# Threshold attention and SwiGLU on one core: two more products by blocks of 128 in the third chunk, and other ranks behind the last scores

## The chip, the cores and the metric

The kernel runs on one core of a Trainium2 chip, in fp32 throughout. The time is that of the device for one launch, in microseconds (us). The core has a matrix engine (PE, with its weight loads shown apart as PEld), three engines for elementwise work (DVE, ACT and POOL), and SP, which only issues DMAs here. Each engine takes its instructions in the order in which the program gives them, and waits for others by semaphores. Matmul results land in PSUM, in eight banks of 128 x 512 fp32; everything else lives in SBUF, 128 partitions wide.

## The reference

```python
# q, k, v: (8, 8, 576, 64)
scores = (1.0 / np.sqrt(64)) * np.matmul(q, k.transpose(0, 1, 3, 2))
thresh = np.max(scores, axis=-1, keepdims=True) - tau
scores = np.where(scores >= thresh, scores, -1000000000.0)
scores = scores - np.max(scores, axis=-1, keepdims=True)
attn = np.exp(scores)
attn = attn / (np.sum(attn, axis=-1, keepdims=True) + 1e-09)
attn_out = np.matmul(attn, v)
x = attn_out.transpose(0, 2, 1, 3).reshape(4608, 512)
g = x @ w_gate                       # (512, 1536)
silu = g * (1.0 / (1.0 + np.exp(-g)))
val = x @ w_val                      # (512, 1536)
out = silu * val @ w_out             # (1536, 512)
```

So per batch there are eight heads of attention with a mask at the row's maximum less tau, and then a feed-forward block over all 4608 tokens.

## The kernel before

**Tokens in chunks.** The feed-forward block works on nine chunks of 512 tokens, `c` = 0 to 8. Chunks 0 to 7 are the first 512 tokens of each batch; chunk 8 (`B` in the code) is made of the last 64 tokens of all batches. The first chunks use plain products, the others seven products in place of eight (Strassen and Winograd forms: sums of the operands' quarters, seven products, sums of these). "Third chunk" is `c` = 2, which the code calls `DEEP`.

**Scores and attention.** Heads go by pairs (`seg`), three tiles of queries to a pair; one tile is one slot, twelve slots to a batch. In a slot `slot_scores` (L2058) writes the scores of a tile into the PSUM tiles `sc`; `slot_rest` then takes the rows' maxima (DVE L2079, L2081), the exponential (ACT L2104), the mask with its row sums (DVE L2106), exchanges sums between partitions (ACT L2115, the job `xj`), adds them up and takes the reciprocal (DVE L2120 and L2121, `rj`), scales six parts (ACT L2133, or POOL L2130 as many times as the table `POOLED` says for this slot) and transposes (DVE L2135). `attend` (L2157) multiplies by v a slot later; PE's next score tile waits for the masks of the one before, since these free the `sc` tiles.

**Gates and values.** While batch b's scores run, `block_part(b, kk)` gives PE the feed-forward work of chunk c = b − 1, so many steps a slot (`GV`). For each of six groups g of 256 columns, `gates_and_values` runs seven products, p1 to p7, of 128 x 128 weights with 256 tokens, four matmuls each (`Group.mul`, L1138). The chunk's two halves of 256 tokens go together: with p3 the first half of the group is complete, with p4 the second, and `finish` then takes tanh and the products with the value. `NestedGroup` does p5 and p3 each as seven products again, of blocks of 128 x 128 tokens (L1333): seven matmuls into two banks, `Seven.fill` (ACT L1271 for 384 columns and L1273 for 512) brings them to SBUF, and `Seven.fold` puts them together with four adds on DVE or POOL, as `FOLDS` says by group (all such adds show as L929 on DVE and L926 on POOL). The weights' sums for it are loaded with the group's other weights, the tokens' sums are made once per chunk by `deepen_x`, four adds on DVE. Which groups take `NestedGroup` is said by `WITH_BLOCKS` = (1, 2, 3) and by the chunk.

**Outputs.** `Deep` multiplies gated values by w_out, again by seven products: `early` and `late` make the sums s1, s2, s3 of the gated values (128x512 each, `sum`), `inner_sums` makes four sums of 128x384 of one operand o for the products inside product o, `nested` is these inner products (L1768, banks px or py), two outer products are flat (L1777). `combine` puts inner products together (four adds big<-big,px on DVE behind an ACT copy), `ship` stores the result (L1829). `deepen(o)` prepares weights, four adds of 128x384 on POOL each.

**Behind the last scores** (`tail[0]` is true) chunks 7 and 8 remain. For each group g the class `Whole` runs the seven products of both chunks, all by blocks (L2543): `folded` brings four of them together on DVE, p3 and p7 add to what `fill` left (DVE L2615, L2625), `fold` runs on POOL, and `finish` takes tanh (ACT L2593), the product with the value (DVE L2595) and an end product by DVE or POOL. Chunk 8's gated values go to HBM (`hall_hbm`, L2608) and are loaded again (L2669) after chunk 7's outputs begin, since their place is still in use. Then the outputs of chunk 7, `Deep(B - 1)`, and of chunk 8, `Deep(B)`, end the kernel.

**The order of the work.** PE's order is the order of the calls. The order on DVE, ACT, POOL and SP is fixed while the program is built, by the class `Plan`: every piece of work is a job with an engine, an estimated duration (`took`), a rank and the jobs that it depends on; at every point of PE's planned time, each engine takes the ready job of least rank, then the one that was ready first. `lag` delays the planned end for those that depend on the job. So a changed rank, lag or engine changes the written order on every engine that follows; the hardware then holds to that order, whatever is ready.

```python
n = min((i for i, j in enumerate(jobs) if j.ready <= start + (0.0 if j.rank else self.PATIENCE)),
        key=lambda i: (self.rank(jobs[i], start), jobs[i].ready, i))
```

Of the kernel before, what the change touches and what calls it, by code (L numbers as in the profile page):

```python
# [14 lines left out]
ALU = mybir.AluOpType  # L15
# [129 lines left out]
def kernel(  # L145
# [13 lines left out]
    B, H, S, D = q.shape  # L159
# [13 lines left out]
    NU3 = 3  # L173
# [4 lines left out]
    NF2, DM2 = NF // 2, DM // 2  # L178
# [50 lines left out]
    NESTED = 0, 1, 6  # L229
# [622 lines left out]
    plan = Plan()  # L852
# [62 lines left out]
    DEEP = 2  # L915
# [345 lines left out]
    class Seven(Buf):  # L1261
# [13 lines left out]
        def fold(self, eng, rank, *deps):  # L1275

            y = self.place.rearrange("p (x q) -> p x q", q=P)
            tt, took, less = (dve_tt, 0.36, 0.23) if eng == "DVE" else (pool_tt, 0.85, 0.52) if tail[0] else (pool_tt, 0.75, 0.44)
            twice = lambda x: y[:, x:x + 1].broadcast_to((P, 2, P))
            j = job(eng, took, tt(y[:, 1:3], twice(0), y[:, 1:3], ALU.add), *deps, rank=rank)  # L1280
            j = job(eng, took, tt(y[:, 0:7:6], twice(2), y[:, 5:7], ALU.add), j, rank=rank)
            j = job(eng, less, tt(y[:, 2], y[:, 0], y[:, 3], ALU.add), j, rank=rank)
            return job(eng, took, tt(y[:, 4:6], twice(6), y[:, 4:6], ALU.add), j, rank=rank)

    class Flat:

# [388 lines left out]
    class Deep:  # L1675
# [37 lines left out]
            self.sixth_place = xall[:, 2 * KW:3 * KW]  # L1713
            self.sixth_sums(mark)

        by_pool = False

        def second_of_s1(self):
            self.by_pool = True
            x = NF2 // 2 - 2  # L1720
            self.ready["s1"].append(self.sum(self.a21, self.a21, self.a22, ALU.add, x, self.ready["s3"][x], gated[self.c, 1, NF2 - 2]))

# [10 lines left out]
        def sum(self, out, a, b, op, x, *deps, rank=2):  # L1733
            fs = slice(2 * x, 2 * x + 2)
            tt, eng, took = (dve_tt, "DVE", 0.62) if tail[0] else (pool_tt, "POOL", 1.3)
            rank = min(rank, 1) if tail[0] else rank
            if self.by_pool and not self.in_outputs:
                tt, eng, took = pool_tt, "POOL", 1.3
            return job(eng, took, tt(out[:, fs], a[:, fs], b[:, fs], op), *deps, rank=rank)

        def inner_sums(self, o, a, place, ready, *deps):

            a11, a21, a12, a22 = quarters(a)
            flat = place if len(place.shape) == 2 else place.rearrange("p f n -> p (f n)")
            s1, s2, s3, s4 = (flat[:, n * QW:(n + 1) * QW].rearrange("p (f q) -> p f q", q=P) for n in range(4))
            tt, eng, took = (dve_tt, "DVE", 0.55) if tail[0] else (pool_tt, "POOL", 1.0)
            rank = 0 if o == 1 and self.c == B - 1 else 0 if o == 1 else 1 if o == 5 or o in (3, 6) and not tail[0] or o in (0, 6) and tail[0] or self.c == B - 2 else 2
            j3 = job(eng, took, tt(s3, a11, a21, ALU.subtract), *ready, *deps, rank=rank)
            j1 = job(eng, took, tt(s1, a21, a22, ALU.add), *ready, *deps, j3, rank=rank)
            j2 = job(eng, took, tt(s2, s1, a11, ALU.subtract), j1, rank=rank)  # L1750
            j4 = job(eng, took, tt(s4, a12, s2, ALU.subtract), j2, rank=rank)
            self.inner[o] = [(a11, ready), (a12, ready), (s4, [j4]), (a22, ready), (s1, [j1]), (s2, [j2]), (s3, [j3])]
# [310 lines left out]
    def slot_rest(seg, t, pss, mark, pooled, max_by_act, rank):  # L2063
# [50 lines left out]
                o = g ^ 1  # L2114
                nc.scalar.copy(sm[g * G:(g + 1) * G, 0:m, 1], sm[o * G:(o + 1) * G, 0:m, 0])  # L2115

        xj = job("ACT", 0.78, exchange, *masks.values(), rank=1)

        def total():
            nc.vector.tensor_reduce(out=tot[:, 0:m], in_=sm[:, 0:m, :], axis=AX.X, op=ALU.add)  # L2120
            nc.vector.reciprocal(out=ri[:, 0:m], in_=tot[:, 0:m])  # L2121

        rj = job("DVE", 0.36, total, xj, rank=1)
        sum_users[-1].append(rj)
        for u in range(NU3):
            scaled = []
# [99 lines left out]
    def gates_and_values(c):  # L2226

        old = None
        settled[0] = c >= DEEP
        while u_bufs[0] is not u_list[0]:  # L2230
            u_bufs.rotate(-1)
        for g in range(NF2):
            deep = c > DEEP and g in WITH_BLOCKS
            new = NestedGroup(c, g) if deep else Group(c, g)
            new.p1(deep or g not in (2, 4))
            yield
            if old is not None:
                old.p4()
                if c >= DEEP and old.g == NF2 - 2:
                    state["deep"].early(plan.t + plan.PIPE)  # L2240
                yield
            for fn in (new.p5, new.p2, new.p6, new.p3, new.p7) if not deep else (new.p2, new.p5, new.p6, new.p3, new.p7):
                fn()
                if c in MORE and fn == (new.p3 if MORE[c] // 4 else new.p2):
                    store_more(c, g)
                if c == DEEP - 1 and fn == new.p5:
                    store_nested(g, plan.t + plan.PIPE)
                if c >= DEEP and g == NF2 - 2 and fn == new.p6:
                    state["deep"] = Deep(c, plan.t + plan.PIPE)
                yield  # L2250
            old = new
        if c == DEEP - 1:
            mark = plan.t + plan.PIPE
            for part in range(2):
                load_flow(c + 1, 0, part, mark, *(j for js in (*plain_stores.values(), *nested_stores.values()) for j in js))
        state["last_product"] = old.p4
# [18 lines left out]
    GV = {1: 3, 2: 6, 3: 4, 4: 6, 5: 7, 6: 3, 7: 5, 8: 7, 9: 0}  # L2275
    GV_FIRST = {1: 5, 2: 8, 3: 2, 4: 5, 5: 7, 6: 2, 7: 5, 8: 7, 9: 0}
    CH = {0: 2, 1: 3, 10: 4, 11: 4}
    POOLED = {0: 3, 1: 1, 2: 1, 3: 3, 4: 3, 5: 2, 6: 1, 7: 2, 8: 1}
    MAX_BY_ACT = (0, 1, 3, 4, 5, 6, 8, 9)
    FIRST_POOLED = {0: 2, 4: 1, 5: 1, 8: 1, 9: 1, 11: 2, 12: 2, 13: 3, 15: 3, 16: 3, 17: 2, 19: 2, 20: 2, 22: 3, 23: 3}  # L2280
    FIRST_MAX_BY_ACT = (1, 3, 6, 9, 10, 11, 12, 13, 14, 18, 20, 21)
# [11 lines left out]
    def block_part(b, kk):  # L2293
# [17 lines left out]
        if kk in GV:  # L2311
            if kk == 1:
                state["gv"], state["c"] = gates_and_values(c), c
                if c > DEEP:
                    deepen_x(c, *(j for js in streamed_kept.values() for j in js))
            gv_steps((GV_FIRST if c == 1 else GV)[kk], kk % NU3 == 0)
            if c == DEEP and kk == 2:
                for o in (4, 2):
                    keep_third(o, plan.t, *summed)
                last_of_sixth(plan.t)  # L2320
                for o in STREAMED:
                    last_of_streamed(o, plan.t)
            if c == DEEP and kk <= len(NESTED):
                deepen(NESTED[kk - 1], plan.t, *(j for js in plain_stores.values() for j in js), *summed)
            if kk == LAST_GV:
                next(state["gv"], None)
                begin_outputs(c)
                if c < DEEP:
                    out_steps(1)
                    end_gates()  # L2330
# [7 lines left out]
    for s, (n, x) in enumerate((n, x) for n in range(len(halved)) for x in range(NU3)):  # L2338
# [20 lines left out]
            store_last(0, j)  # L2359
        if s == 1:  # L2360
            prepare_v(seg)
        at_, pooled, max_by_act = (kk, POOLED, MAX_BY_ACT) if b > DEEP else (s, FIRST_POOLED, FIRST_MAX_BY_ACT)
        slot_rest(seg, t, pss, mark, pooled.get(at_, 0), at_ in max_by_act, 1 if x == NU3 - 1 else 2)
        if x == 1 and n > 0:
            for place, load in held:
# [270 lines left out]
    for g in range(NF2):  # L2636
        for c in (B - 1, B):
# [10 lines left out]
            for fn in (new.p2, new.p6, new.p3, new.p7) if old is not None else (new.p5, new.p2, new.p6, new.p3, new.p7):  # L2648
                fn()
                if (c, g) == (B, NF2 - 1) and fn == new.p2:  # L2650
                    state["deep"].sums_of_last(plan.t + plan.PIPE)
                if (c, g) == (B, NF2 - 1) and fn == new.p6:
                    state["deep"].late(plan.t + plan.PIPE)
            old = new
    state["last_product"] = old.p4
    begin_outputs(B - 1)
# [56 lines left out]
```

## Time and profile before

| what | value |
|---|---|
| median of 3 runs | 1343.5 us (1342.71 to 1345.19) |
| the profiled execution | 1344.29 us |
| its span in the profile | 1342.4 us |
| PE busy | 1327.0 us, 16274 matmul records |
| DVE, ACT, POOL busy | 1082.9, 899.1, 932.8 us |
| mean granted clock of PE | 0.999 |
| last scores end, last attend begins | about 1126 us |
| products of `Whole` | 1136 to 1275 us |

Times in the views count from the start of the span; the profiled execution has 1.9 us outside it. An fp32 matmul leaves two records in the trace, so a product of four matmuls shows as "x8". A timeline row has the start, the time from its first start to its last end, engine, line, operation, the tiles by name (out<-in) with shape and number of instructions, and in brackets how long the engine stood idle before it and what ended that. Records of matmuls overlap at their ends, so the pitch from one product's start to the next one's is what a product costs.

### The profile page before, as it was taken

The numbers are of one execution on the slowest core, as the hardware profiler recorded it, in microseconds if no ns is written. First come the engines' busy times: TensorE is split into PE (matmuls) and PEld (weight loads), VectorE is DVE, ScalarE is ACT, GpSimd is POOL, SyncE is SP. The second block draws the span as 40 slices with busy tenths as digits, with TensorE's granted clock in tenths as the row PEclk, the third lists the DMA queues.
The fourth block names the chain that finished last, engine by engine and source line by source line (L and its number), as shares of the span: only waits on it lengthen the run. The fifth ranks groups of instructions, "written<-read, shape, count | busy, mean of one in ns | idle before, by whom it ended". The sixth has DMA issues, their size and how long they took to land. (4 is left out here: it accounts for less than half of the span.)

```text
span 1342.4 us, 41686 instructions
## 1 busy us (share of the span) xinstructions
PE 1327.0 (99%) x16274; PEld 1123.1 (84%) x16274; DVE 1082.9 (81%) x2891; ACT 899.1 (67%) x2341; POOL 932.8 (69%) x1115
## 2 busy tenths in 40 slices
PE   9999999999999999999999999999999999999998
PEld 7777877787887878888888888888888889999998
DVE  7888898888887778888888887888888887667886
ACT  6888777767756677787777777777777775344300
POOL 2688497565685759857895779677976799856720
PEclk9999999999999999999999999999999999999999
DMA  8852424356557553656365746655474627565241
GB/s 180 205 188 92 85 58 134 122 150 178 154 166 220 174 167 89 208 165 219 76 201 168 232 111 187 178 168 149 115 214 146 213 68 232 158 202 183 88 169 40
DMA packets 230884, 209.81 MB, mean 156 GB/s; under 512 B 167968, under 2 KB 185376, under 8 KB 223008
## 3 DMA queue, kind: packets, MB, share of 16 engines
q1 hardware_dynamic: 226768, 206.22, 52.2%
q8 instruction: 129, 2.11, 0.7%
q10 hardware_dynamic: 3920, 0.92, 0.3%
q14 instruction: 67, 0.55, 0.1%
HBM read 169.08 MB, written 38.01 MB: 154 GB/s over the span
## 5 line engine op out<-in xcount | busy, mean ns | idle before, releaser
L2106 DVE SCALAR_TENSOR_TENSOR pall<-sc,th,pall 128x288 f32<-128x288 f32 x504 | 244.2, 513 | 42.6 <-ACT pall L2104 23.4
L2104 ACT ACTIVATE pall<-sc,nm 128x288 f32<-128x288 f32 x504 | 232.9, 498 | 35.3 <-DVE pall L2106 34.9
L2135 DVE STREAM_TRANSPOSE pall<-pall 128x576 f32<-128x576 f32 x252 | 188.3, 764 | 22.1 <-ACT pall L2133 12.1
L1138 PE MATMUL pb<-xall,big 128*128 128x256 f32 x864 | 205.8, 381 | 0.0
L2133 ACT ACTIVATE pall<-pall,ri 128x288 f32<-128x288 f32 x388 | 178.9, 527 | 27.7 <-DVE ri L2121 26.9
L926 POOL TENSOR_TENSOR big<-big 128x128 f32<-128x128 f32 (+3 forms) x214 | 158.9, 751 | 46.5 <-ACT big L1273 20.8
L1138 PEld LDWEIGHTS pb<-xall,big 128*128 128x128 f32 x864 | 161.2, 190 | 24.0 <-issue 2.2
L926 POOL TENSOR_TENSOR hall<-hall,tmp 128x512 f32<-128x512 f32 x80 | 102.3, 1279 | 95.6 <-DVE hall L1197 75.9
L2079 DVE TENSOR_REDUCE mx<-sc 128x2 f32<-128x576 f32 x168 | 125.7, 748 | 39.7 <-PE sc L2058 39.3
L2058 PE MATMUL sc<-kT,qT 64*32 64x288 f32 (+1 forms) x5376 | 145.3, 345 | 0.4 <-DVE pall L2106 0.4
L1138 PE MATMUL pa<-xall,big 128*128 128x256 f32 x576 | 137.7, 382 | 0.0
L2058 PEld LDWEIGHTS sc<-kT,qT 64*32 64x32 f32 x5376 | 96.2, 106 | 48.6 <-issue 9.3
L2157 PE MATMUL xa<-pall,vall 64*32 64x288 f32 x4032 | 129.4, 404 | 0.5 <-PE px L1768 0.4
L1138 PEld LDWEIGHTS pa<-xall,big 128*128 128x128 f32 x576 | 107.8, 190 | 17.5 <-issue 2.5
L2157 PEld LDWEIGHTS xa<-pall,vall 64*32 64x32 f32 x4032 | 75.6, 107 | 46.6 <-issue 5.0
L2130 POOL TENSOR_SCALAR pall<-pall,ri 128x288 f32<-128x288 f32 x116 | 58.2, 513 | 53.1 <-DVE ri L2121 52.8
L1138 PE MATMUL pe<-xall,big 128*128 128x256 f32 x384 | 91.4, 381 | 0.0
L2115 ACT COPY sums<-sums 32x6 f32<-32x6 f32 x336 | 66.6, 198 | 30.3 <-DVE pall L2106 25.2
L1138 PEld LDWEIGHTS pe<-xall,big 128*128 128x128 f32 x384 | 72.4, 190 | 11.1 <-ACT pall L2133 0.7
L2081 DVE TENSOR_REDUCE mx<-sc 128x1 f32<-128x288 f32 x168 | 75.0, 447 | 0.0
L926 POOL TENSOR_TENSOR hall<-hall 128x384 f32<-128x384 f32 (+2 forms) x69 | 70.0, 1028 | 0.8
L1196 ACT ACTIVATE vall<-tmp 128x512 f32<-128x512 f32 x72 | 45.1, 627 | 35.6 <-POOL tmp L926 19.0
(365 smaller groups left out, 3051.6 us busy)
## 6 DMA issues: line engine op xcount, KB each, us to landing
big<-sums_hbm SPq DMA_DIRECT2D x30, 1280.0 KB, 7.9
big<-sums_hbm SPq DMA_DIRECT2D x30, 1024.0 KB, 7.8
vall<-in_v_dram SPq DMA_DIRECT2D x112, 144.0 KB, 3.5
big<-sums_hbm SPq DMA_DIRECT2D x54, 256.0 KB, 3.6
sums_hbm<-big SPq DMA_DIRECT2D x36, 256.0 KB, 3.8
out_dram<-big SPq DMA_DIRECT2D x32, 256.0 KB, 2.8
qT<-in_q_dram SPq DMA_DIRECT2D x112, 72.0 KB, 4.0
kT<-in_k_dram SPq DMA_DIRECT2D x112, 72.0 KB, 3.0
```

Of the source, the lines that this page charges most:

```text
L926: return lambda: nc.gpsimd.tensor_tensor(out=out, in0=a, in1=b, op=op)
L1138: nc.tensor.matmul(ps[:, i], w[:, k_, i * P:(i + 1) * P], x[:, k_, :], start=first and i == k_ == 0, stop=True, skip_group_check=True)
L2058: nc.tensor.matmul(pss[h][(slice(g * G, (g + 1) * G), *part)], qT[hs, col:col + G], kT[hs, c * SH + keys[0]:c * SH + keys[1]], start=True, ...
L2079: rs.append(job("DVE", 0.72, lambda n=n, tile_=tile_: nc.vector.tensor_reduce(out=mx[:, n:n + 2, 0], in_=tile_[:, :, 0:SH], axis=AX.X, op= ...
L2081: rs.append(job("DVE", 0.42, lambda n=n, tile_=tile_: nc.vector.tensor_reduce(out=mx[:, n + 2:n + 3, 0], in_=tile_[:, :, SH:SH + SQ], axis ...
L2104: ej = job("ACT", 0.42, lambda x=x, n=n: nc.scalar.activation(ps[x], scs[x], AF.Exp, bias=nm[:, n:n + 1]), ej, masks.get((h, u - 1)), rank=0)
L2106: masks[x] = job("DVE", 0.45, lambda x=x, n=n: nc.vector.scalar_tensor_tensor(out=ps[x], in0=scs[x], scalar=th[:, n:n + 1], in1=ps[x], op0 ...
L2115: nc.scalar.copy(sm[g * G:(g + 1) * G, 0:m, 1], sm[o * G:(o + 1) * G, 0:m, 0])
L2130: scaled.append(job("POOL", 0.48 if seg["i"] >= 3 * NP else 0.4, lambda x=x, n=n: nc.gpsimd.tensor_scalar(out=x, in0=x, scalar1=ri[:, n:n ...
L2133: scaled.append(job("ACT", 0.46, lambda x=x, n=n: nc.scalar.activation(x, x, AF.Copy, scale=ri[:, n:n + 1]), rj, rank=rank))
L2135: seg["turned"].append(job("DVE", 0.72, lambda both=both: nc.vector.transpose(out=both, in_=both), *scaled, rank=rank))
L2157: nc.tensor.matmul(holds[a].ap()[x * G:(x + 1) * G, 0:SH].rearrange("d (i q) -> d i q", q=G), vr[rs, h, j, ds], p[rs, h, :, j, :], start=( ...
```

## The change

- p5 and p3 of groups 1 to 3 of chunk 2 are done by `NestedGroup` too (`c >= DEEP`), and `deepen_x` runs for chunk 2. The jobs of `deepen`, which prepare three operands of w_out on POOL, are given in slots 4 to 6 of chunk 2 and no longer in slots 1 to 3.
- `Seven.fold`'s last job counts as ending 0.6 later for what depends on it, behind the last scores.
- The five 128x512 sums of `Deep(B - 1)` that come last (two of s1, three of s2) run on DVE and no longer on POOL, and the call that issued s1's last and s2's three after p6 of the last group is gone; they are issued with the end of the gates.
- `inner_sums` gets other ranks: operand 6 of chunk 8 goes to 0, operand 1 behind the last scores to 1 for chunk 8.
- The very last score tile's exchange and total get rank −1, and two of its six scalings go to POOL.

```diff
@@ Seven.fold
-            return job(eng, took, tt(y[:, 4:6], twice(6), y[:, 4:6], ALU.add), j, rank=rank)
+            return job(eng, took, tt(y[:, 4:6], twice(6), y[:, 4:6], ALU.add), j, rank=rank, lag=0.6 if tail[0] else 0.0)
@@ Deep
-        by_pool = False
-
         def second_of_s1(self):
-            self.by_pool = True
             x = NF2 // 2 - 2
...
@@ Deep.sum
             tt, eng, took = (dve_tt, "DVE", 0.62) if tail[0] else (pool_tt, "POOL", 1.3)
             rank = min(rank, 1) if tail[0] else rank
-            if self.by_pool and not self.in_outputs:
-                tt, eng, took = pool_tt, "POOL", 1.3
@@ Deep.inner_sums
-            rank = 0 if o == 1 and self.c == B - 1 else 0 if o == 1 else 1 if o == 5 or o in (3, 6) and not tail[0] or o in (0, 6) and tail[0] or self.c == B - 2 else 2
+            rank = 0 if o == 6 and self.c == B else 0 if o == 1 and self.c == B - 1 else 1 if o == 1 and tail[0] else 0 if o == 1 else 1 if o == 5 or o in (3, 6) and not tail[0] or o in (0, 6) and tail[0] or self.c == B - 2 else 2
@@ slot_rest
-        xj = job("ACT", 0.78, exchange, *masks.values(), rank=1)
+        first = -1 if seg is halved[-1] and t == seg["tiles"][-1] else 1
+        xj = job("ACT", 0.78, exchange, *masks.values(), rank=first)
...
-        rj = job("DVE", 0.36, total, xj, rank=1)
+        rj = job("DVE", 0.36, total, xj, rank=first)
@@ gates_and_values
-            deep = c > DEEP and g in WITH_BLOCKS
+            deep = c >= DEEP and g in WITH_BLOCKS
@@
-    POOLED = {0: 3, 1: 1, 2: 1, 3: 3, 4: 3, 5: 2, 6: 1, 7: 2, 8: 1}
+    POOLED = {NS: 2, 0: 3, 1: 1, 2: 1, 3: 3, 4: 3, 5: 2, 6: 1, 7: 2, 8: 1}
@@ block_part
-                if c > DEEP:
+                if c >= DEEP:
                     deepen_x(c, *(j for js in streamed_kept.values() for j in js))
...
-            if c == DEEP and kk <= len(NESTED):
-                deepen(NESTED[kk - 1], plan.t, *(j for js in plain_stores.values() for j in js), *summed)
+            if c == DEEP and 4 <= kk < 4 + len(NESTED):
+                deepen(NESTED[kk - 4], plan.t, *(j for js in plain_stores.values() for j in js), *summed)
@@ the loop over slots
-        at_, pooled, max_by_act = (kk, POOLED, MAX_BY_ACT) if b > DEEP else (s, FIRST_POOLED, FIRST_MAX_BY_ACT)
+        at_, pooled, max_by_act = (kk if n + 1 < len(halved) or x + 1 < NU3 else NS, POOLED, MAX_BY_ACT) if b > DEEP else (s, FIRST_POOLED, FIRST_MAX_BY_ACT)
@@ behind the last scores, after each product
-                if (c, g) == (B, NF2 - 1) and fn == new.p6:
-                    state["deep"].late(plan.t + plan.PIPE)
```

## The prediction

> **What bounds the kernel now.** I read the busy rows first, then the windows, then what TensorE (PE) waits for, then each engine's timeline where the change touches it.
>
> ```profile
> PE 1327.0 (99%) x16274; PEld 1123.1 (84%) x16274; DVE 1082.9 (81%) x2891; ACT 899.1 (67%) x2341; POOL 932.8 (69%) x1115
> ```
>
> PE is busy for all but 15 us of the span. The windows say where the gaps are:
>
> ```profile
> 400.00:500.00 100.00, 100.00 (x1280) 79.77 (x1279) 74.11 (x217) 68.02 (x187) 65.27 (x87) 1.00 0.65 193
> 1100.00:1200.00 100.00, 99.05 (x1071) 97.19 (x1056) 71.08 (x174) 46.18 (x113) 80.13 (x108) 1.00 0.59 182
> 1200.00:1300.00 100.00, 99.06 (x841) 97.58 (x841) 76.12 (x140) 31.51 (x69) 58.29 (x69) 1.00 0.48 159
> ```
>
> Columns: the stretch, its length, busy time of PE, PEld, DVE, ACT and POOL, the granted clock. In the third chunk (about 420 to 510) PE never pauses, so PE time saved there counts in full unless a new wait eats it. Behind the last scores (1126 on) PE pauses 0.9 us per 100 us, and there the order of DVE's jobs matters. The waits of PE (total, times, longest) name those pauses:
>
> ```profile
> PE sc L2543 <- DVE tmp L2625: 0.9, 1, 0.9
> PE px L1768 <- DVE big L929: 0.9, 1, 0.9
> PE sc L2543 <- ACT tmp L1273: 0.5, 1, 0.5
> PE xa L2157 <- PE px L1768: 0.4, 1, 0.4
> ```
>
> **The change part by part.** The sum runs against the profiled execution, 1344.29 us (span 1342.4 and 1.9 outside it), 0.8 above the median of 1343.5.
>
> *1. Six products by blocks (p5 and p3 of groups 1 to 3, chunk 2).* PE's timeline has both forms:
>
> ```profile
> 452.71 1.89 PE L1138 MATMUL pe<-xall,big 128*128 128x256 f32 x8
> 454.44 1.89 PE L1138 MATMUL pa<-xall,big 128*128 128x256 f32 x8
> ...
> 584.38 0.61 PE L1333 MATMUL pe<-xall,big 128*128 128x128 f32 x4
> ...
> 585.94 1.89 PE L1138 MATMUL pb<-xall,big 128*128 128x256 f32 x8
> ```
>
> A plain product (4 matmuls, 8 records) starts 454.44 − 452.71 = 1.73 us before its successor; one of 7 block matmuls takes 585.94 − 584.38 = 1.56. Six times 0.17: **−1.0 us**, all on the path. That is small because 7 × 128 columns against 4 × 256 saves an eighth of the streaming at most (−0.22).
>
> The blocks also load more weights: 14 load records of 0.192 us (2.69 us) a product against 8 of 0.190 (1.52). As 1.56 us holds all seven pairs in chunk 3, they lie beside matmuls and cost nothing. Would each stand open, a product would cost 1.17 − 0.17 = +1.0, all six +6. The Trainium skill (TensorE: Matmul & The Clock Gate, "Part 3: Packing small matmuls — row/col tiling") says that a weight load overlaps matmuls in flight only when it goes to other row groups; by that rule the +6 would hold, which this trace does not bear out, and the measurement decides.
>
> What the blocks add elsewhere, from their rows in chunk 3:
> - ACT: per product a fill of 0.48 (L1271) beside the 0.60 (L1273) that replaces L1161's 0.60: +2.9 us on an engine 68% busy there.
> - Folds: four adds of 0.42, 0.42, 0.28, 0.42 on DVE (two of six products) or 0.73, 0.73, 0.46, 0.73 on POOL (four): +3.0 on DVE, +10.5 on POOL, with 20 to 35 us idle per 100. Four adds of `deepen_x` (up to 0.84 each) join DVE once. The g1 add (0.68) replaces L1209's 0.69: nothing.
> - The moved `deepen`: twelve POOL adds of 1.0 us go from slots 1–3 to slots 4–6. Their weights are first read by the outputs at 511.09; slot 6 issues the last four some 20 us earlier, behind all other ranks on POOL, which idles for 25 us in 450:500 (the window shows 28.8 busy after 36.5 in 400:450, where they are now). No DMA is among them. Nothing; were the cover gone, each late add would cost 1.0.
>
> All of it is cover until a fold delays score masks. Around one tile of chunk 2 the last mask (L2106) started at 444.80 and the next score matmul at 447.52: about 2.2 us of slack. A DVE fold takes 1.35 of it; two-input SBUF adds on DVE stretch to about 1.6 beside POOL's adds (rows below), so the slack can just go. I take **+0.5**, between 0 and 1.5 (one late tile at each of three groups, 0.5 each).
>
> *2. The last score tile.* Its exchange and total now go first, and two of six normalisations to POOL. Before:
>
> ```profile
> 1121.78 0.69 DVE L2018 TENSOR_TENSOR vall<-py,vall 128x512 f32<-128x512 f32 x1 [1.28 <-PE py L1768]
> 1122.39 0.55 DVE L2020 TENSOR_TENSOR vall<-py,vall 128x384 f32<-128x384 f32 x1
> 1122.85 0.16 DVE L2120 TENSOR_REDUCE tot<-sums 128x6 f32<-128x18 f32 x1
> ```
>
> The total waited behind two adds though its sums were there at 1121.36; the transposes end late and the last attend starts 0.42 late. **−0.4**; nothing less, since PE follows PE behind it.
>
> *3. Start of the whole products (1137).* The last combine of chunk 6's outputs (four adds big<-big,px) ran between qT and xall sums; in the new order three of those sums (0.62 and 0.41) come ahead. The next product's copy (L2557) and PE's third product at 1139.50 have no slack. 0 (if DVE, started earlier by part 2, has finished them) to +2 (all sums and their stretch): I take **+1.5**, as these sums are not ready early.
>
> *4. Fold's last job gets lag 0.6.* In ACT's new order the next fills (L1271, L1273) go ahead of tanh (L2593, 0.63). At 1166.13 the fill behind tanh made PE wait 0.5: **−0.5**. POOL's end products come one place later; they feed sums due later, nothing.
>
> *5. The five 128x512 sums of s1 and s2, POOL to DVE, and when they are issued.* DVE at the end of the whole products, before:
>
> ```profile
> 1270.15 1.57 DVE L929 TENSOR_TENSOR big<-hall,big 128x384 f32<-128x384 f32 x1
> 1271.65 1.14 DVE L2625 SCALAR_TENSOR_TENSOR tmp<-sc,tmp 128x512 f32<-128x512 f32 x2
> ...
> 1275.83 1.51 DVE L929 TENSOR_TENSOR xall<-big,xall 128x384 f32<-128x384 f32 x1
> ...
> 1283.97 0.68 DVE L929 TENSOR_TENSOR hall<-hall,big 128x512 f32<-128x512 f32 x1
> 1284.58 1.62 DVE L929 TENSOR_TENSOR big<-big 128x384 f32<-128x384 f32 x1
> ```
>
> (1.5 to 1.6 is a 128x384 add beside a POOL add; alone it is 0.55.) In the new order an add less stands before L2625, so it starts 0.8 earlier and PE's stall there (0.9) goes: **−0.9**.
>
> But s4 of o=6 (xall<-big,xall, before at 1275.83) now stands behind the last L2595, the three s2 sums and the four adds of p2's combine. From L2625's end to s4's end: three 384 sums (0.56, 0.55, 0.55), a 512 sum beside POOL (1.23), two 384 sums (1.08, 0.65), L2595 (1.21), four folded adds with a 512 sum (2.5), L2595 (0.69), three s2 sums (two at 0.68, one beside POOL 1.6), four px adds (1.64), s4 (0.55): 14.3, less 17 overlaps of 0.08 between records, 12.9. L2625's end moves to 1272.7 − 0.8 = 1271.9, so s4 ends at 1284.8. PE reads it in the product that began at 1283.22, now 0.9 earlier: 1282.3. **+2.5**, between 0 (these sums drained in DVE's earlier idle places) and 4.3 (all three s2 sums at 1.6).
>
> *6. SP's order.* The combine of p2 moves ahead, so its output store, and the reload of hall queued behind it on SP, go some 3.5 us earlier:
>
> ```profile
> 1288.26 0.39 SPq L1829 DMA_DIRECT2D out_dram<-big  x1
> ...
> 1289.26 0.86 SPq L2669 DMA_DIRECT2D xall<-hall_hbm  x2
> ```
>
> The reload landed at 1295.72, and from there DVE ran without a gap to the sum that PE awaited at 1313.41. **−0.9**, that wait. The new ranks of chunk 8's operands 6 and 1 only reorder sums inside that chain of DVE: 0, between ∓0.6, one 384 sum more or less ahead of a product. The tail behind PE's end (1338.79 to 1342.4) is untouched. Chunk 6's last store goes a few DMAs later on SP; nobody reads it. The hall_hbm stores, one pair later, are due only at the reload: nothing.
>
> Sum: −1.0 + 0.5 − 0.4 + 1.5 − 0.5 − 0.9 + 2.5 − 0.9 = **+0.8**: 1345.1 profiled, **1344.3** against the median.
>
> **The rivals.**
> - *The s4 wait is hidden* (faster): s2's sums or s4 slip into DVE's idle places, and as DVE then runs ahead, part 3 costs nothing either. −1.0 + 0.5 − 0.4 + 0 − 0.5 − 0.9 + 0 − 0.9 = −3.2: 1340.3. For it: DVE is 24% idle in 1200:1300. Against: s4's place on DVE is written, behind nine jobs that are themselves late, though its input is ready long before.
> - *The s4 wait is long* (slower): all three s2 sums stretch beside POOL (4.3), and one 384 sum more takes 1.6 in place of 0.55: a wait of 5.35, +3.65 in all, 1347.1. It decides from a wait of 4.5 on. For it: DVE rows of 1.5 to 1.6 between 1270 and 1284. Against: POOL, relieved of five sums, adds less there.
> - *Nothing shows:* the parts behind the last scores only shift slack, because DVE's chain from the reload to 1313 sets the end; then −1.0 + 0.5 remain, 1343.0. Against: four different waits of PE stand in the list.
> - *The loads don't overlap:* +6 in place of −1.0, 1351.3. Against: the pitch of 1.56. The rule of the Trainium skill named above would have it so.
>
> **How the numbers follow.** My forecast (about ±1 around +0.8) 0.45, hidden 0.24, nothing shows 0.13, long wait 0.17, loads 0.01. 0.2% is 2.7 us, about what a measurement of this kernel tells from no change. Of the hidden case, spread around −3.2, 0.16 lies beyond it; of the long wait 0.16; the forecast gives 0.02 on the fast and 0.03 on the slow side. Faster 0.18, same 0.62, slower 0.20. The range reaches to the hidden case's value and to a wait of 5.2, leaving out about 1 in 10 on each side: 1340.3 to 1347.0.
>
> **What would show it.** PE's pitch around L1333 in chunk 2 at 1.56, and windows of 400:500 with no less than 99.5 busy (part 1); no wait of PE at L2157, and L2120 ahead of L2018 (2); a wait of PE or a gap before L2557 near 1137 (3); no wait on L1273 near 1166 (4); no wait on L2625, but a wait of PE L1768 on DVE xall of 2.5 near 1281 (5); the reload issued near 1286 and no wait near 1313 (6). A PE wait on masks in chunk 2, or none on xall, makes the number wrong.

## The result, and the profile after

The changed kernel takes 1347.14 us (median; 1344.50 to 1349.39), the kernel before 1343.69 on the same chip (1342.61 to 1345.89): a ratio of 1.0026, interval 1.0019 to 1.0033, so 3.45 us slower. The forecast was +0.8. The profiled execution of the changed kernel took 1348.85, its span is 1347.0; against the 1342.4 of before that is 4.6.

The busy row and the windows of the changed kernel, the three stretches shown of before and two short ones more (columns as before: the stretch, its length, busy time of PE, PEld, DVE, ACT and POOL, granted clock, DMA share, GB/s):

```profile
PE 1328.7 (99%) x16310; PEld 1123.7 (83%) x16310; DVE 1095.7 (81%) x2908; ACT 902.1 (67%) x2348; POOL 940.7 (70%) x1128
```

```profile
400.00:500.00 100.00, 99.99 (x1313) 80.95 (x1314) 79.89 (x228) 69.76 (x190) 75.35 (x100) 1.00 0.63 185
1100.00:1200.00 100.00, 98.58 (x1111) 94.17 (x1094) 70.78 (x169) 45.33 (x112) 82.59 (x111) 1.00 0.55 174
1200.00:1300.00 100.00, 97.69 (x835) 96.31 (x834) 81.11 (x149) 33.16 (x72) 54.86 (x65) 0.98 0.50 168
1284.00:1288.00 4.00, 1.69 (x15) 1.50 (x14) 3.90 (x9) 0.00 (x0) 0.00 (x0) 0.98 0.27 98
1288.00:1292.00 4.00, 4.00 (x13) 3.29 (x13) 3.93 (x8) 0.97 (x2) 0.00 (x0) 0.60 1.00 311
```

PE is busy for 1.7 us more than before, though the six products save 1.0. The third column from the end is the clock: PE idles for 2.3 of the 4 us from 1284 on, and in the next 4 us it is granted 0.60 of its speed on the mean (finer windows, in the last section, show 0.50 for 3.41 us). Slow matmuls count as busy time. What PE waits for (total, times, longest), and PE behind the wait (a row's start, its length, what it does, in brackets the idle time before it and its releaser):

```profile
PE px L1763 <- DVE xall L929: 2.3, 1, 2.3
PE pa L2539 <- ACT pb L2553: 1.3, 1, 1.3
```

```profile
1287.21 1.12 PE L1763 MATMUL px<-extra,xall 128*128 128x128 f32 x6 [2.31 <-DVE xall L929]
1288.13 6.88 PE L1772 MATMUL py<-wo,hall 128*128 128x256 f32 x24
```

DVE comes to s4 (the third row) behind the three s2 sums and the adds of p2's combine:

```profile
1282.17 2.96 DVE L929 TENSOR_TENSOR big<-hall,big 128x512 f32<-128x512 f32 x3
1285.05 1.64 DVE L929 TENSOR_TENSOR big<-big,px 128x256 f32<-128x256 f32 x4
1286.61 0.55 DVE L929 TENSOR_TENSOR xall<-big,xall 128x384 f32<-128x384 f32 x1
```

The four waits shown of before are gone: L2625, L1273, the one near 1313, and that of the last attend. In their place stand the wait for s4 (`xall`) of 2.31, and one of 1.31 near 1142 in the second product pair behind the last attend. The flat product of 24 records behind the s4 wait lasts 6.88; before it lasted 5.34, and its twin further on in this kernel 5.35.

PE executes the same calls in both kernels but for the six products, so the difference of the start times of equal PE matmuls, changed less before, says where time was lost (two profiled executions):

| stretch | predicted | measured |
|---|---|---|
| head, same code in both | 0 | +2.2 |
| 420 to 511: six products and score waits | −1.0 + 0.5 | +0.42 |
| 511 to 1100, unchanged code | 0 | −0.76 |
| last attend | −0.4 | +0.19 |
| 1131 to 1267, with the 1.31 wait and L1273 | +1.5 − 0.5 | +0.68 |
| L2625, near 1272 | −0.9 | −1.20 |
| s4 wait | +2.5 | +2.58 |
| clock behind it | not in the sum | +1.68 |
| near 1313 | −0.9 | −1.17 |

The head's 2.2 is no part of the change: the clock of 0.57 to 0.60 from 8 to 12 us that makes most of it (1.3) stands in six of the fourteen profiled executions, one of them of the kernel before with nothing but a made pause far behind (below); the rest is a score wait near 141, 1.28 long in place of 0.38, also ahead of anything that the change touches. The −0.76 is a loss near 1061 in the profile of before: the changed kernel and five others looked at do without it, the kernel before with the lag alone among them. Without the two the column gives +3.2, near the measured 3.45. The last attend lost its wait of 0.42, but lasts 5.37 where it lasted 4.70 (PE before, then in the changed kernel):

```profile
1126.85 4.70 PE L2157 MATMUL xa<-pall,vall 64*32 64x288 f32 x144 [0.42 <-PE px L1768]
```

```profile
1128.21 5.37 PE L2153 MATMUL xa<-pall,vall 64*32 64x288 f32 x144
```

In chunk 2 a product by blocks costs what was predicted, 1.56 (443.17 less 441.61):

```profile
441.61 0.61 PE L1333 MATMUL pe<-xall,big 128*128 128x128 f32 x4
...
443.17 1.89 PE L1138 MATMUL pb<-xall,big 128*128 128x256 f32 x8
```

But the score rows grew; the one near 485, on PE's timeline before and then in the changed kernel:

```profile
485.05 1.70 PE L2058 MATMUL sc<-kT,qT 64*32 64x288 f32 x64
```

```profile
486.89 2.45 PE L2053 MATMUL sc<-kT,qT 64*32 64x288 f32 x64
```

The same 64 records take 0.75 more, without an idle time of PE that the list of waits names. The last of the masks (0.52 long) that free the `sc` tiles began at 483.77 before, 1.28 ahead of the scores, and at 486.88 in the changed kernel, with them: the last scores go as the masks end.

### The profile page after: what moved, and what is told of

It is laid out like the page before. It is cut to its first block, busy times and chain, and to the rows that moved or that the text cites. A ratio compares the mean times of both kernels' runs of the same rounds, so it can differ in the third digit from the quotient of the medians.

```text
span 1347.0 us, 41770 instructions
## 1 busy us (share of the span) xinstructions
PE 1328.7 (99%) x16310; PEld 1123.7 (83%) x16310; DVE 1095.7 (81%) x2908; ACT 902.1 (67%) x2348; POOL 940.7 (70%) x1128
## 4 chain that ended last, share of the span: by engine, by line
PE 88%; DVE 4%; POOL 4%; DMA 2%; ACT 1%; issue 1%; DVEq 0%; POOLq 0%; ACTq 0%; SPq 0%
PE pb L1138 14%; PE sc L2053 10%; PE pa L1138 9%; PE px L1763 9%; PE xa L2153 9%; PE po L1446 6%; PE pe L1138 5%; PE sc L2539 5%; PE pe L1333 4%; PE pb L2539 3%; PE py L1763 3%; PE pv L1371 2%; PE pg L1371 2%; PE py L1772 2%; PE pa L2539 2%; PE sc L484 1%
## 5 line engine op out<-in xcount | busy, mean ns | idle before, releaser
L926 POOL TENSOR_TENSOR big<-big 128x128 f32<-128x128 f32 (+3 forms) x230 | 170.9, 752 | 62.5 <-ACT big L1273 23.7
L1138 PE MATMUL pe<-xall,big 128*128 128x256 f32 x336 | 80.1, 381 | 0.0
L1138 PEld LDWEIGHTS pe<-xall,big 128*128 128x128 f32 x336 | 63.3, 190 | 9.9 <-ACT xlast L2165 0.9
L926 POOL TENSOR_TENSOR tmp<-tmp 128x256 f32<-128x256 f32 (+3 forms) x53 | 51.2, 977 | 28.5 <-DVE tmp L2611 11.8
```

The lines of the kernel that those rows point to most:

```text
L926: return lambda: nc.gpsimd.tensor_tensor(out=out, in0=a, in1=b, op=op)
L1138: nc.tensor.matmul(ps[:, i], w[:, k_, i * P:(i + 1) * P], x[:, k_, :], start=first and i == k_ == 0, stop=True, skip_group_check=True)
```

## The experiments

Four questions were open. Does the low clock come of the s4 pause, or would the pause have cost the same without it? Is the 1.31 wait the cost of the sums put ahead of the combine, or of something else? Why did the last attend not get shorter? And why does chunk 2 lose instead of gain? Each ratio is against the kernel before, on the same chip in the same session. Only the kernels with idle matmuls or a made pause add work, whose result nobody uses.

**s4 ahead of the s2 sums** (changed kernel, one rank):

```diff
-            j4 = job(eng, took, tt(s4, a12, s2, ALU.subtract), j2, rank=rank)
+            j4 = job(eng, took, tt(s4, a12, s2, ALU.subtract), j2, rank=0 if o == 6 and self.c == B - 1 else rank)
```

> The changed kernel (1347.1) with one job moved: s4 of operand 6 of chunk 7's outputs gets rank 0 and comes right behind s2, as before the change; the orders of PE, ACT, POOL and SP stay. Clock theory: PE's pause of 2.5 us ahead of the product that reads s4 costs its length and then a spell of low granted clock (0.60 in 1288 to 1292 of the profile, flat half in 6.88 instead of 5.34, so 1.5 to 1.8 us). Both go: about 1343.0, clock 1.00 there in the profile. Rival, wait alone (the low clock was chance, as at the head of the same profile): 2.5 go, 1344.6. Rival, the loss is in chunk 2's score waits: at most 1.5 of 3.45 go, 1345.6 or more.

1344.89 us, ratio 1.0006 (0.9997 to 1.0014): 2.7 less than the changed kernel by the ratios. By the number alone this is nearer to the rival "wait alone" (1344.6) than to the clock theory (1343.0); the trace shows why. The s4 wait is gone and the clock stays at 1.00, but PE stops in the flat product right behind it. PE's timeline in this kernel:

```profile
1285.13 0.83 PE L1763 MATMUL px<-extra,xall 128*128 128x128 f32 x6
1287.27 4.99 PE L1772 MATMUL py<-wo,hall 128*128 128x256 f32 x22 [1.30 <-DVE big L929]
```

The flat product writes the bank py, which the combine of p2 must have read; that combine now stands behind the s2 sums. Of 2.58 + 1.68 lost at this place, the new order wins back all but 1.30, and it has a longer gap in the last attend (0.95).

**Idle matmuls in the pause.** Matmuls of 128x256 that nobody reads, in the bank py, ahead of the product that needs s4; five, then two (changed kernel):

```diff
-            m = self.m7 = self.nested(6, x, True, *deps)
+            m = self.m7 = self.nested(6, x, True, *deps, to=6 if self.c == B - 1 else NQ)
+            if self.c == B - 1:
+                self.y = y = take("py")
+                pe(0.0, lambda: [nc.tensor.matmul(y.ap()[:, 0:DM2], operands[0][:, 0, 0:P], operands[0][:, 0, :], start=True, stop=True,
+                                                  skip_group_check=True) for _ in range(2)], *y.deps)
+                m = self.m7 = self.nested(6, x, False, *deps, lo=6)
```

> The changed kernel with five idle matmuls (128x256, 0.43 us each, into a bank that is written anew later) ahead of the product that waits for s4; all else in the same order. The wait for s4 stays as long, but PE is idle for only some 0.3 us of it. Clock theory: granted clock stays 1.00 and 1.5 to 1.8 us go: about 1345.4. Wait alone: nothing goes, 1347.1, or a little more if the idle matmuls end late.

With five: 1347.03, 1.0022 (1.0012 to 1.0032). The idle matmuls waited for their own bank for 1.50 and then ended after s4 was there, so PE came 3.90 late in place of 2.58. The clock stayed at 1.00, but as the lateness changed with it, this run separates nothing. With two:

> As fill, with two idle matmuls (0.86 us) in place of five: they wait 1.5 for their bank, run, and s4 is then due, so PE's last inner product of p7 starts as late as in the changed kernel, but PE's longest pause is 1.5. Clock theory: clock 1.00 behind it, 0.8 to 1.6 less than the changed kernel: 1345.6 to 1346.4. Wait alone: 1347.1.

1345.98, 1.0015 (1.0006 to 1.0024). PE's timeline and the two short windows of the kernel with two idle matmuls:

```profile
1285.20 1.10 PE L1991 MATMUL py<-wo 128*128 128x256 f32 x4 [1.51 <-DVE big L929]
1286.14 0.83 PE L1763 MATMUL px<-extra,xall 128*128 128x128 f32 x6
```

```profile
1284.00:1288.00 4.00, 2.80 (x16) 2.51 (x17) 3.90 (x9) 0.97 (x2) 0.00 (x0) 1.00 0.48 145
1288.00:1292.00 4.00, 4.00 (x21) 3.51 (x20) 3.86 (x8) 0.00 (x0) 0.00 (x0) 1.00 1.01 357
```

The product that waits for s4 is as late as in the changed kernel (2.61 against 2.58), yet the pause ahead of it is split, at most 1.51 long, and the clock behind it is 1.00. It is 1.2 us faster than the changed kernel (1.5 by the ratios), as the clock theory expected, though the two intervals overlap. The lateness of PE and the low clock behind it are thus two costs; the changed kernel's trace has them apart as 2.58 and 1.68.

**A pause alone** (kernel before). PE waits for a copy that ACT makes, at the same place, ahead of the last inner product; k further copies set the length, 1 and 3:

```diff
+                def pause():
+                    t, w = self.spaces[3], operands[0]
+                    nc.scalar.copy(t[:, 0:P], x[0].ap()[:, 2 * P:3 * P])
+                    for _ in range(k):
+                        nc.scalar.copy(t[:, 0:512].rearrange("p (a b) -> p a b", a=2), w[:, 0:2, :])
+                    nc.tensor.matmul(y.ap()[:, 0:P], t[:, 0:P], w[:, 0, 0:P], start=True, stop=True, skip_group_check=True)
```

> The kernel before, with a pause of PE put in ahead of the last inner product of p7 in chunk 7's outputs: a small idle matmul there waits for two copies on ACT that begin when the inner product ahead is done. All else in the same order. Pause of about 1.2 us. Clock theory (a pause of over some 2 us lets the granted clock fall): the granted clock stays 1.00 behind it, time +1.2 less what slack behind it takes up: 1344.3 to 1345.5.

> As pause1 with four copies, a pause of about 2.4 us, as long as the wait for s4 in the changed kernel. Clock theory: the granted clock falls to about 0.6 for some 4 us behind it in most executions, so the time rises by 2.4 and another 1.5: 1346.5 to 1348. Rival, wait alone: 1345.5 to 1346.7, clock 1.00.

k = 1: a pause of 1.00, clock 1.00 behind it, 1344.69, ratio 1.0006 (0.9997 to 1.0015). k = 3, PE's timeline and window:

```profile
1286.17 0.49 PE L2002 MATMUL sc<-wo,pall 128*128 128x128 f32 x2 [2.31 <-ACT pall L2001]
```

```profile
1288.00:1292.00 4.00, 4.00 (x20) 3.51 (x20) 2.27 (x5) 0.39 (x2) 0.00 (x0) 1.00 0.65 170
```

1346.38, 1.0017 (1.0008 to 1.0026). The pause is as long as in the changed kernel, 2.31, and in this execution the clock behind it is 1.00. In two of its eleven executions the mean granted clock is 0.997, in the rest 0.998 to 1.000. So a pause of 2.3 us does not always lower the clock; the last section shows what it depends on. In both runs the wait near 1313 vanished (−1.17): a later PE finds the sum ready.

**Part 1 alone** (kernel before with the blocks in chunk 2 and the moved `deepen`):

```diff
-            deep = c > DEEP and g in WITH_BLOCKS
+            deep = c >= DEEP and g in WITH_BLOCKS
...
-                if c > DEEP:
+                if c >= DEEP:
...
-            if c == DEEP and kk <= len(NESTED):
-                deepen(NESTED[kk - 1], plan.t, *(j for js in plain_stores.values() for j in js), *summed)
+            if c == DEEP and 4 <= kk < 4 + len(NESTED):
+                deepen(NESTED[kk - 4], plan.t, *(j for js in plain_stores.values() for j in js), *summed)
```

> The kernel before with part 1 alone: six products by blocks in chunk 2, the twelve POOL adds in slots 4 to 6; nothing behind chunk 2 changes its order. Clock theory: -1.0 from the six products, +1.3 from the score waits seen in the profile: 1344.0. Rival, chunk 2 makes the loss: 1345.5 or more. If the score wait was chance: 1342.7.

1347.02, 1.0018 (1.0006 to 1.0030): part 1 is a loss of its own. Chunk 2 costs +0.4, as in every kernel that has part 1, and then a gap appears 600 us later, in code that part 1 does not touch. PE's timeline of this kernel at the last attend:

```profile
1128.82 4.68 PE L2157 MATMUL xa<-pall,vall 64*32 64x288 f32 x141 [0.42 <-PE px L1768]
1134.99 0.67 PE L2157 MATMUL xa<-pall,vall 64*32 64x288 f32 x3 [1.48 <-issue]
```

Three records from its end PE stands for 1.48 us, and "issue" says that it waited for nothing that the profile shows. The profile has two DMA queues of kind "instruction"; on the one with more bytes a packet of 16 KB ran from 1132.36 to 1133.38, and PE went on 1.6 us behind its end. The attend ended 2.1 later than before.

**Seventy-two instructions more** (kernel before). Part 1 gives PE 36 matmul and 36 load records more. If the gap comes of where a block of instructions ends, any 72 more ahead of it must do; so the idle matmuls that begin the program become 24 in place of 6:

```diff
-    def run_idle(n):
+    def run_idle(n, small=0):
...
+        for _ in range(small):
+            nc.tensor.matmul(ps[:, 0:32], ones[:, 0:P], ones[:, 0:32], start=True, stop=True)
...
-    run_idle(6)
+    run_idle(3, 21)
```

> The kernel before, with 18 more matmuls in the idle warm-up at the head (3 of 128x256 and 21 of 128x32 instead of 6 of 128x256): 72 more PE instructions ahead of everything, as many as part 1 adds in chunk 2; all else in the same order. Code theory: all four kernels with part 1 have a gap in the middle of the last attend (0.1 to 1.5 us, released by nothing) right behind the load of an instruction block, none of those without part 1 has it; 72 more instructions move the block's border into the attend, so the gap appears here too, near record 140 of 144, and the time rises by 0.5 to 1.5: 1345 to 1346. Rival, part 1's own work (fold, POOL adds, DMAs) delays something that the last attend needs: no gap, 1344.3 as the kernel before.

1350.89, 1.0052 (1.0035 to 1.0069). Of this, 6.1 is the head itself, where the small matmuls ran longer than meant. The attend, 1100 us later, in the same code as before:

```profile
1132.08 4.65 PE L2159 MATMUL xa<-pall,vall 64*32 64x288 f32 x139 [0.42 <-PE px L1770]
1137.85 0.68 PE L2159 MATMUL xa<-pall,vall 64*32 64x288 f32 x5 [1.12 <-issue]
```

The gap is there, without blocks or moved jobs. Over all profiles it stands in eight of eight kernels with 72 PE instructions more ahead of it (0.11 to 1.68 us) and in none of the six without; in all eight PE goes on 1.3 to 1.6 us behind the end of such a packet. That PE waits for instructions is what this fits, not shown directly: the stretch has 288 records in 4.7 us, with the DMA engines full (part 1 alone: share 0.91 to 1.03 from 1124 to 1132, ten weight loads); that these loads delay the instructions was not tried.

**The changed kernel without part 1:**

> The changed kernel without part 1, so only the ranks, lag and homes behind the last scores. Clock theory: nearly the whole loss stays, 1346.8. Rival, chunk 2 makes the loss: 1345.2 or less.

Its edit is the diff of part 1 the other way round. 1347.32, 1.0023 (1.0013 to 1.0033). No gap in the attend, but the wait near 1142 is now 4.05 long. DVE's timeline of this kernel, and PE's:

```profile
1140.22 1.73 DVE L929 TENSOR_TENSOR big<-big,px 128x256 f32<-128x256 f32 x4 [3.26 <-DMA out_dram<-big]
```

```profile
1142.22 1.22 PE L2539 MATMUL pa<-xall,big 128*128 128x128 f32 x4 [4.05 <-ACT pb L2553]
```

DVE is idle for 3.26 and waits for a store of the outputs; behind PE's wait the clock is at 0.50 for 6.83 us. The losses of the two, 2.4 and 3.1 by their ratios, add up to more than 3.45. That a PE which is late from the gap waits less at 1142 (1.31 in place of 4.05) fits this, but was not tried by itself.

**Why the combine waits.** The block `big` that it writes is one that an earlier store reads. In the changed kernel DVE's row is:

```profile
1140.90 1.72 DVE L929 TENSOR_TENSOR big<-big,px 128x256 f32<-128x256 f32 x4 [0.98 <-DMA out_dram<-big]
```

SP's timeline before, then of the changed kernel:

```profile
1130.94 1.72 SPq L1829 DMA_DIRECT2D out_dram<-big  x2
1132.76 0.41 SPq L2399 DMA_DIRECT2D pall<-last_hbm  x1
```

```profile
1132.39 0.37 SPq L2395 DMA_DIRECT2D pall<-last_hbm  x1
...
1134.80 0.90 SPq L1824 DMA_DIRECT2D out_dram<-big  x2
```

Part 2 put the load of `last_hbm`, which waits for the last attend, and four weight loads ahead of the two stores: they begin at 1134.80 in place of 1130.94. The store that DVE waits for, that of the block which POOL combines, went at 1130.94 and landed 2.2 later before the change; now it goes at 1135.28, 1.5 behind POOL's last add, and lands 5.5 later. Two kernels were to test it. First, the stores ahead of the loads on SP (changed kernel):

```diff
-            ob_jobs[n] = [job("SP", 0.1, fn, j, lag=2.8)]
+            ob_jobs[n] = [job("SP", 0.1, fn, j, rank=0 if tail[0] else 1, lag=2.8)]
```

> The changed kernel with one edit: output stores get rank 0 on SP behind the last scores. One store of chunk 6 goes ahead of three weight loads; PE, DVE, ACT and POOL keep their orders. Store theory: at 1137 to 1142 DVE's adds big<-big,px wait for that store (its block is written anew), 1.0 us in the changed kernel's profile, 3.3 in the one without part 1. The store goes some 1.5 us earlier, so the wait of DVE on out_dram shrinks by as much and PE's wait on the copy L2553 falls from 1.3 towards 0: about 1346.0. Rival, the step as predicted (the sums for qT and xall ahead of the adds hold them up): nothing changes, 1347.1.

1347.46, 1.0027 (1.0017 to 1.0037): nothing won; DVE is idle for 2.03, and PE's gap is 1.54. But the edit moved the wrong store, as SP's and DVE's timelines of this kernel show:

```profile
1133.03 0.39 SPq L1824 DMA_DIRECT2D out_dram<-big  x1
...
1135.95 0.39 SPq L1824 DMA_DIRECT2D out_dram<-big  x1
```

```profile
1140.47 1.72 DVE L929 TENSOR_TENSOR big<-big,px 128x256 f32<-128x256 f32 x4 [2.03 <-DMA out_dram<-big]
```

The store at 1133.03 is that of the block which DVE combines. DVE's next combine waits for the other: its block was complete when POOL's last add ended at 1132.26, yet it stood on SP behind three weight loads until 1135.95 and landed 4.4 later. So this run does not rule out SP's order as the cause; it left the store that counts where it was. The two added scalings (0.99) also end POOL's combine 1.0 later against PE than before, in the changed kernel. Second, part 2 left out:

```diff
-        first = -1 if seg is halved[-1] and t == seg["tiles"][-1] else 1
+        first = 1
...
-    POOLED = {NS: 2, 0: 3, 1: 1, 2: 1, 3: 3, 4: 3, 5: 2, 6: 1, 7: 2, 8: 1}
+    POOLED = {0: 3, 1: 1, 2: 1, 3: 3, 4: 3, 5: 2, 6: 1, 7: 2, 8: 1}
```

> The changed kernel without part 2: the last tile's exchange and total back at rank 1, its six scalings all on ACT. Store theory: with part 2 POOL does two scalings first and finishes chunk 6's third combine later, and the plan puts its output store behind the load that waits for the last attend; the fourth combine, which writes the same block anew, then waits for that store and PE's third whole product for the combine's copy (1.3 here, 1.5 with the store moved on SP alone, 4.1 without part 1). Without part 2 stores go as before: no wait of DVE on out_dram, PE's wait on L2553 gone, the 0.4 ahead of the last attend back, so 0.9 less and fewer spells of low clock: 1345.5 to 1346.2. Rival, part 3 of the prediction (other sums ahead of the adds): PE's wait stays 1.0 or more, 1347 to 1347.6.

1349.51, 1.0038 (1.0026 to 1.0051): slower, against what was expected. The wait near 1142 and DVE's wait for a store are both gone (the stores go at 1131.24 again), so part 2 makes them. As the three sums of qT and xall go back behind the combine's first adds too, this run does not part store and sums; in the changed kernel DVE idles behind these sums until the store lands, so the store is what ends last there. But the gap in the attend is at its longest, and the clock falls behind it. PE's timeline and the window of this kernel:

```profile
1133.54 0.67 PE L2153 MATMUL xa<-pall,vall 64*32 64x288 f32 x3 [1.68 <-issue]
1134.14 2.42 PE L1763 MATMUL px<-wo,hall 128*128 128x128 f32 x12
```

```profile
1134.00:1138.00 4.00, 4.00 (x21) 3.86 (x21) 2.81 (x7) 0.85 (x4) 1.87 (x4) 0.59 0.99 302
```

The twelve records take 2.42; before and in the changed kernel they take 1.60. The s4 pause of 2.32 lowers the clock a second time, to 0.57.

**The lag alone** (kernel before with the last job of `fold` 0.6 later behind the last scores):

```diff
-            return job(eng, took, tt(y[:, 4:6], twice(6), y[:, 4:6], ALU.add), j, rank=rank)
+            return job(eng, took, tt(y[:, 4:6], twice(6), y[:, 4:6], ALU.add), j, rank=rank, lag=0.6 if tail[0] else 0.0)
```

> The kernel before with part 4 alone, the lag of fold's last job. The fills go ahead of tanh, so PE's wait of 0.5 on L1273 near 1166 is gone; the waits on L2625 and at 1313 stay: 0.5 less, 1343.5 on this chip, or no change where the wait at 1272 grows by it.

1344.57, 1.0002 (0.9993 to 1.0011). The wait on L1273 (0.5) is gone as predicted, and PE's list of waits shows where it went, with 0.9 and 0.9 in these rows before:

```profile
PE px L1768 <- DVE big L929: 2.2, 1, 2.2
PE sc L2543 <- DVE tmp L2625: 1.4, 1, 1.4
```

At L2625 DVE is ready only 0.3 earlier, and a PE that is 0.7 early waits there. Near 1313 DVE's chain ends 1.06 later in this execution: the reload was issued 0.53 later and landed 1.07 later.

**What is left when the losing parts go** (changed kernel without parts 1 and 2, with s4 first; the edits are those above):

> The changed kernel without parts 1 and 2 and with s4 right behind s2: only the lag and the homes and ranks of the sums are left. Theory: -0.5 at 1166 and -0.9 at 1272, then a wait of PE of about 1.3 at the flat product for its PSUM bank (freed by p2's combine, which stands behind the three s2 sums), which the missing wait at 1313 (0.9) repays: 1343.0 to 1343.6, against 1344 of the kernel before on this chip. If the five sums on DVE cost more than they free, 1344.5.

1342.56, 0.9991 (0.9982 to 1.0000): 4.7 us faster than the change as made, by the ratios, and 1.2 below the kernel before, where the interval reaches to 1.0000, so that a win over it is not shown. The waits on L2625, L1273 and near 1313 are gone, and the 1.30 on the bank py stands in their place; the wait near 1142 is absent here too.

## Why the prediction was wrong

Between the +0.8 of the forecast and the +3.2 of the table, the clock makes +1.7, chunk 2 +0.9, the last attend +0.6, and the other rows −0.8 together.

- **The term "+2.5" for s4 had a part missing, and this is the largest error: the step that failed.** Place, cause and size of the wait were right (2.31 in the wait list, +2.58 in PE's start times; from L2625's end to s4's end 13.2 in place of 12.9, the listed pieces adding to 14.2 and not 14.3). But the term priced the pause alone, "between 0 … and 4.3", with the clock at 1.00 all along. The pause lowers the clock to 0.50 for 3.41 us, +1.68. Of the changed kernel's executions, the two with a mean clock of 1.000 took 1344.5 each, close to the forecast; the five at 0.997 took 1347.1 to 1349.4. The mean over its executions is 0.9981, that of the kernel before in the later runs 0.9993 to 0.9994: 0.0012 × 1343 = 1.6 us (falls at the head of the program counted in), of a miss of 2.65 (+3.45 against +0.8).
- **"All of it is cover until a fold delays score masks": the term was too small.** The products gained the −1.0. But the score rows that wait for late masks stretched by 0.44 near 450 and by 0.75 near 487, and the attend ahead of the first by 0.2: +1.4 in place of +0.5, so chunk 2 lost 0.4. PE was still 99.99% busy there; the sign that the forecast chose could not show it. DVE's busy time in 400:500 rose from 74.11 to 79.89, POOL's from 65.27 to 75.35: the slack of 2.2 "can just go", and it went.
- **Six products, "all on the path", left out what 72 instructions more do far behind them.** With them PE stands still in the densest stretch of the program, most likely for want of instructions. In the changed kernel the last attend grew by 0.6, so part 2's "−0.4" became +0.19; in others the gap is up to 1.68.
- **"+1.5" at 1137 had the right size, 1.31, and a wrong cause.** The sums of qT and xall did go first, but what DVE then waits for is a store. Part 6 looked at chunk 6's last store alone, which "goes a few DMAs later on SP; nobody reads it". The store that counts is one of the two ahead of it: nobody reads its block, but the next combine writes it.
- **Right:** the pitch of the products, the attend's own wait (−0.4), L1273, L2625 (−1.20 for −0.9), the wait near 1313 (−1.17 for −0.9, gone with a later PE too, as the pauses show). Left out: behind s4 the text saw nothing more that PE would wait for there; the flat product's bank, 1.30, is the next.
- **The rivals.** "The s4 wait is long" gave 1347.1, the time that was measured, by a wait of 5.35 that did not occur. A rival that hits the number is not confirmed by it.

What stays open: how much of the 3.45 each part bears when they interact, whether the gap in the attend is a wait for instructions, and what counts as idle for the clock (below).

## What to carry over

Where the clock falls behind idle windows, price a new pause of PE by its length and by what the clock may cost behind it: here 2.3 us of pause cost 1.7 more in the executions in which it fell into one window. When a store moves later, look for the next writer of its block, not only for readers of the result. A gain on a wait counts only if the chain that ends next has slack: take the lag alone, which won 0.5 at one wait and gave it back at the next two.

## What the runs showed that was not expected

*The clock falls by windows of 3.41 us.* The trace records the granted clock as stretches of 1.00 and 0.50. In all fourteen profiles, every border between them lies on a grid of 3.413 us, to 0.003; where the grid lies differs from execution to execution. Each row below is one cell of the grid (columns as before): in the changed kernel the one that holds the s4 pause and the next; in the kernel before with the made pause (k = 3) the two that the pause falls into and the next.

```profile
1284.41:1287.82 3.41, 1.10 (x10) 0.91 (x9) 3.31 (x9) 0.00 (x0) 0.00 (x0) 1.00 0.26 97
1287.82:1291.24 3.42, 3.42 (x11) 2.79 (x11) 3.35 (x7) 0.97 (x2) 0.00 (x0) 0.50 1.01 295
```

```profile
1281.38:1284.80 3.42, 2.49 (x23) 2.29 (x21) 3.39 (x7) 1.40 (x4) 0.11 (x1) 1.00 0.08 28
1284.80:1288.21 3.41, 2.04 (x13) 1.94 (x14) 3.34 (x6) 2.04 (x5) 1.47 (x1) 1.00 0.22 79
1288.21:1291.62 3.41, 3.41 (x17) 3.00 (x17) 2.06 (x5) 0.18 (x1) 0.00 (x0) 1.00 0.64 184
```

Both pauses are 2.31 long. The first lies in one cell, and the next cell is granted 0.50; the second is cut by a border, at most 1.37 in one cell, and the clock stays. The pauses of PE at the places named:

| kernel, place | pause, us | most of it in one cell | clock in the next cell |
|---|---|---|---|
| before with a made pause (k = 1), s4 | 1.00 | 0.99 | 1.00 |
| s4 first, flat product | 1.30 | 1.30 | 1.00 |
| five idle matmuls, s4 | 1.50 | 1.50 | 1.00 |
| two idle matmuls, s4 | 1.51 | 0.97 | 1.00 |
| without part 2, last attend | 1.68 | 1.68 | 0.50 |
| changed kernel, s4 | 2.31 | 2.31 | 0.50 |
| before with a made pause (k = 3), s4 | 2.31 | 1.37 | 1.00 |
| stores first, s4 | 2.31 | 2.31 | 0.50 |
| without part 2, s4 | 2.32 | 2.32 | 0.50 |
| without part 1, s4 | 2.32 | 1.73 | 1.00 |
| the lag alone, near 1313 | 2.23 | 1.77 | 1.00 |
| without part 1, near 1142 | 4.05 | 2.25 | 0.50, for two cells |

So the same pause lowers the clock or not by where the grid happens to lie. Among the products of 128x128 the clock fell where a cell held 2.25 of pause or more, and not with 1.77 or less. In the last attend, whose matmuls show as 64*32, 1.68 was enough: the time without a matmul alone does not decide, and no run here shows what does. One cell at 0.50 cost 1.68 in the changed kernel, about half of its length. It follows that the profile of the two idle matmuls says little by itself, as a border would have cut a whole pause there too; what speaks for them is the time over eleven executions.

The Trainium skill (TensorE: Matmul & The Clock Gate, "Part 1: The HAM clock gate (the "warmup" mystery)") speaks of a free-running window of some 3.4 us and of idle gaps above that length as those to avoid. The trace agrees with the window: 3.413 us, with a grid that lies differently in each execution. The length does not agree, since 1.68 and 2.31 within one window were enough here, and the measurement decides.

*PE stands still in a dense stretch,* and 72 instructions at the head decide whether it does so 1100 us later (1.12 us with them, none without; one profile each).
